# Convolution of the first two steps moved from VectorE and GpSimd to TensorE, with another order of all instructions

## The chip, the cores and the metric

The kernel runs on one core of one Trainium2 chip. The time is the device time of one execution in microseconds (us). Engines: PE is TensorE (PEld its weight loads), DVE is VectorE, ACT is ScalarE, POOL is GpSimd, SP is SyncE, whose queue issues nearly all transfers.

## The reference

Windowed attention with sinks, then a gated block with a causal convolution of five taps, all in float32. B = 4, H = 8, S = 768, head size 64, model size 512, 4 sinks, window 128.

```python
scores = where(is_sink | in_window, q @ k.T / 8, -1e9)
a = exp(scores - max(scores)); a = a / (sum(a) + 1e-9)
x = a @ v                                   # heads side by side: (B, S, 512)
gate_pre[s] = sum(conv_w[k] * x[s - 4 + k] for k in range(5))   # zeros ahead of s = 0
out = (sigmoid(gate_pre) * (x @ w_val)) @ w_out
```

w_val, w_out and conv_w arrive as float64 and are decoded on the chip into a high and a low float32 part.

## The kernel before

The work is cut into 24 steps s (batch, third of 256 positions, half of the heads) and 12 pairs m of two steps. A step's attention output is `xt`, 128 channels x 2 halves x 256 positions. What runs in which order on every engine is written out by hand: `ORDER` is a list of event names such as `s0.3` (name, then step, pair or weight chunk), and the program calls the function of each name in that order. Each engine runs its own instructions strictly in that order.

Events that matter here, with their lines in the kernel before: `kq`, `vv` load a step's k and q, and its v (L234 to L247); `wvl`, `wol` load a weight chunk, and `wva` to `wvf` decode it (ACT L135, L154, L149, L181, DVE, POOL L155, and three matmuls on PE, L176 to L178, the weight sum). `s0`, `s1` are the score groups of a step (PE L373, then DVE); `e0`, `e1` their exps on ACT (L397); `rec`, `norm` divide by the sums (POOL L412); `tx` transposes the probabilities (PE L434), `px`, `py` mask and copy them; `sk`, `ts` do the same for the sinks (PE L439); `vl`, `si` are the value products (PE L491, L500). `xc` copies the step's output from PSUM to `xt` (ACT L507), `xh`, `xl` make its high and low part. `c4` multiplies by the last tap (POOL L528), `hd` writes the four positions ahead of the tile into PSUM (ACT L519), `c0`, `c1` add two taps each (DVE L536, one instruction for each tap and half), `th` is the tanh (ACT L541). Per pair, `v0` to `v3` multiply with w_val (PE L555), `g`, `h`, `l` make the gated product and its parts, `o0` to `o3` multiply with w_out (PE L606), `t` stores. `fill` are dummy products of zeros on PE (L222), four in an event.

PSUM has two pairs of score banks, pr_86 and pr_87, used in turn by score groups and transposes (`pair`); two accumulators ac_92 and ac_93, used in turn by dummies, weight sums, sink transposes, `v` and `o` (`homes`); and one bank pair xv for the value products. A user waits until the last reader of its bank is done. For steps with p = 0 (the first two of a batch) the exps read a masked copy in SBUF (`sx`), for the others they read the score bank itself. `scalars` loads n_sink and window, `flag` tests them with eight small DVE operations; the result selects, after the main program, a general path that does not run here.

Of the kernel before, what the change touches and what calls it, by code (L numbers as in the profile page):

```python
# [41 lines left out]
sk.1 c1.0 wvf.2 wol.2 e1.3 ts.1 sk.2 px.2 vl.1 rec.3 th.0 woe.1 si.1 xc.1 xh.1 hd.1 wvd.3 s0.4 c4.1 wof.1 c0.1
fill.4g py.2 vv.10 wve.3 woa.2 ts.2 xl.1 woa.3 norm.3 e0.4 c1.1 s1.4 vv.2 wod.1 wvf.3 wob.2 v0.0 wob.3 v1.0 vv.5
tx.3 vl.2 vv.3 y0.0 th.1 v2.0 g0.0 hd.2 py.3 woe.3 h0.0 si.2 e1.4 l0.0 xc.2 v3.0 wod.3 o2.0 px.3 woe.2 y1.0 g1.0
c4.2 rec.4 kq.8 h1.0 wod.2 s0.6 xh.2 e0.6 wof.2 l1.0 s0.5 c0.2 o0.0 wof.3 c1.2 s1.6 o3.0 t1.0 e0.5 o1.0 xl.2 norm.4
sk.3 ts.3 vl.3 si.3 t0.0 kq.7 xc.3 xh.3 tx.4 hd.3 s1.5 sk.4 ts.4 px.4 e1.5 xl.3 v0.1 c4.3 v1.1 rec.5 py.4 v2.1 vv.4
c0.3 y0.1 th.2 c1.3 g0.1 e1.6 v3.1 y1.1 s1.7 s0.7 norm.5 th.3 vl.4 h0.1 l0.1 e1.7 si.4 tx.5 kq.9 rec.6 sk.5 xc.4
o0.1 kq.12 ts.5 g1.1 px.5 hd.4 s1.8 h1.1 o2.1 c4.4 l1.1 xh.4 c0.4 e0.7 o1.1 norm.6 xl.4 o3.1 t0.1 sk.6 vv.7 c1.4
rec.7 py.5 norm.7 tx.6 px.6 vl.5 e1.8 si.5 ts.6 t1.1 py.6 xh.5 xc.5 s0.9 s0.8 xl.5 vv.6 c4.5 sk.7 v0.2 hd.5 ts.7
th.4 e0.9 v1.2 sv.7 c0.5 v2.2 tx.7 c1.5 e0.8 rec.8 sv.6 g0.2 py.7 s1.9 px.7 v3.2 kq.10 th.5 vl.6 h0.2 s1.10 si.6  # L50
e1.9 norm.8 g1.2 xc.6 xh.6 hd.6 l0.2 rec.9 c4.6 tx.8 o0.2 vv.8 h1.2 l1.2 o2.2 xl.6 c0.6 py.8 c1.6 px.8 e1.10 o3.2
# [796 lines left out]
```

## Time and profile before

| | us |
|---|---|
| median of 3 runs (lowest, highest) | 268.03 (268.02, 268.99) |
| the profiled execution | 267.36 |
| its span in the profile | 265.6 |
| PE busy | 250.7 (94%) |
| DVE busy | 207.1 (78%) |
| ACT busy | 185.5 (70%) |
| POOL busy | 177.8 (67%) |

The span runs from the first to the last instruction that the profiler recorded; the execution's own time is 1.76 us longer. Matmuls are pipelined: a record's length includes the way through the array, so the time that one takes of PE is read from start to start of a long series, not from a record's length. A float32 matmul shows as two records.

### The profile page before, as it was taken

The numbers are of one execution on the slowest core, as the hardware profiler recorded it, in microseconds if no ns is written. First come the engines' busy times: TensorE is split into PE (matmuls) and PEld (weight loads), VectorE is DVE, ScalarE is ACT, GpSimd is POOL, SyncE is SP. The second block draws the span as 40 slices with busy tenths as digits, with TensorE's granted clock in tenths as the row PEclk, the third lists the DMA queues.
The fourth block names the chain that finished last, engine by engine and source line by source line (L and its number), as shares of the span: only waits on it lengthen the run. The fifth ranks groups of instructions, "written<-read, shape, count | busy, mean of one in ns | idle before, by whom it ended". The sixth has DMA issues, their size and how long they took to land. (4 is left out here: it accounts for less than half of the span.)

```text
span 265.6 us, 11978 instructions
## 1 busy us (share of the span) xinstructions
PE 250.7 (94%) x4978; PEld 207.6 (78%) x4978; DVE 207.1 (78%) x579; ACT 185.5 (70%) x686; POOL 177.8 (67%) x234
## 2 busy tenths in 40 slices
PE   7877999999999998999999999999999999999991
PEld 2345469769888877979888889999889889798991
DVE  6999999958979798888797878977689968953330
ACT  3899988868978767586657688587585566555131
POOL 3489987785696882885883786795692766676130
PEclk9999999999999999999999999999999999999999
DMA  6998771328335232763327636335055213020202
GB/s 203 329 364 236 246 264 39 127 86 265 107 118 168 63 122 84 251 228 116 89 79 232 211 99 207 94 107 165 9 160 174 63 42 102 2 81 2 81 3 88
DMA packets 27548, 36.57 MB, mean 138 GB/s; under 512 B 2272, under 2 KB 24032, under 8 KB 27488
## 3 DMA queue, kind: packets, MB, share of 16 engines
q1 hardware_dynamic: 27344, 35.62, 42.0%
q8 instruction: 41, 0.67, 1.1%
q14 instruction: 19, 0.16, 0.2%
q10 hardware_dynamic: 144, 0.13, 0.2%
HBM read 29.45 MB, written 6.29 MB: 135 GB/s over the span
## 5 line engine op out<-in xcount | busy, mean ns | idle before, releaser
L536 DVE SCALAR_TENSOR_TENSOR sg<-xv,cw,sg 128x256 f32<-128x256 f32 x192 | 77.7, 475 | 7.0 <-POOL sg L528 6.3
L412 POOL TENSOR_TENSOR wx<-w,sm 128x512 f32<-128x512 f32 x48 | 49.1, 1043 | 4.6 <-DVE sm L404 4.2
L555 PE MATMUL ac<-xh,wvh 128*128 128x256 f32 x192 | 49.5, 291 | 1.1 <-DVE pr L378 1.1
L584 POOL TENSOR_TENSOR gl<-sg,gh 128x512 fp32r<-128x512 f32 x24 | 30.9, 1291 | 29.1 <-ACT gh L580 29.0
L555 PE MATMUL ac<-xh,wvl 128*128 128x256 f32 x192 | 48.0, 283 | 0.0
L397 ACT ACTIVATE w<-pr,ngm 128x132 f32<-128x132 f32 x128 | 45.7, 369 | 1.7
L373 PE MATMUL pr<-k,q 64*32 64x168 f32 (+2 forms) x1536 | 36.7, 301 | 4.3 <-DMA q<-in_qt_dram 1.4
L528 POOL TENSOR_TENSOR sg<-xt,cw 128x512 f32<-128x512 f32 x24 | 25.5, 1063 | 20.8 <-ACT xt L507 20.7
L606 PE MATMUL ac<-woh,gh 128*128 128x512 f32 (+1 forms) x96 | 39.0, 406 | 0.0
L555 PEld LDWEIGHTS ac<-xh,wvh 128*128 128x128 f32 x192 | 36.9, 192 | 1.7 <-issue 0.5
L555 PEld LDWEIGHTS ac<-xh,wvl 128*128 128x128 f32 x192 | 36.7, 191 | 1.1 <-issue 1.0
L606 PE MATMUL ac<-wol,gh 128*128 128x512 f32 (+1 forms) x96 | 37.3, 388 | 0.0
L491 PE MATMUL xv<-wt,v 64*32 64x192 f32 (+2 forms) x2048 | 36.3, 275 | 1.0 <-PE ac L439 0.8
L606 PE MATMUL ac<-woh,gl 128*128 128x512 f32 (+1 forms) x96 | 37.2, 387 | 0.0
L491 PEld LDWEIGHTS xv<-wt,v 64*32 64x32 f32 x2048 | 33.7, 105 | 3.7 <-issue 1.5
L373 PEld LDWEIGHTS pr<-k,q 64*32 64x32 f32 x1536 | 23.9, 106 | 12.5 <-issue 3.2
L378 DVE COPY_PREDICATED pr<-low,pr 128x256 f32<-128x256 uint8 x48 | 20.3, 423 | 15.4 <-PE pr L373 14.5
L523 POOL TENSOR_TENSOR xl<-xt,xh 128x512 fp32r<-128x512 f32 x24 | 30.8, 1287 | 1.7 <-ACT xh L515 1.6
L555 PE MATMUL ac<-xl,wvh 128*128 128x256 f32 x192 | 30.9, 283 | 0.0
L555 PEld LDWEIGHTS ac<-xl,wvh 128*128 128x128 f32 x192 | 26.5, 192 | 0.0
L397 ACT ACTIVATE w<-sx,ngm 128x132 f32<-128x132 f32 x64 | 25.0, 400 | 1.9 <-DVE ngm L387 1.9
L397 ACT ACTIVATION_READ_ACCUMULATOR w<-pr,ngm 128x1 f32 x128 | 26.0, 203 | 0.0
(124 smaller groups left out, 460.6 us busy)
## 6 DMA issues: line engine op xcount, KB each, us to landing
k<-in_kt_dram SPq DMA_DIRECT2D x23, 408.0 KB, 5.3
v<-in_vt_dram SPq DMA_DIRECT2D x16, 384.0 KB, 4.5
q<-in_qt_dram SPq DMA_DIRECT2D x23, 256.0 KB, 5.3
out_dram<-osb SPq DMA_DIRECT2D x23, 256.0 KB, 2.6
raw<-in_w_val_dram SPq DMA_DIRECT2D x4, 512.0 KB, 5.8
v<-in_vt_dram SPq DMA_DIRECT2D x8, 256.0 KB, 3.9
raw<-in_w_out_dram SPq DMA_DIRECT2D x4, 512.0 KB, 5.9
vs<-in_vsk_dram SPq DMA_DIRECT2D x8, 64.0 KB, 3.5
```

The source lines that it names most:

```text
L373: nc.tensor.matmul(ss[e * QB:(e + 1) * QB, j, c * n + x0:c * n + x1], q[js, g, (4 * c + e) * QB:(4 * c + e + 1) * QB], k[js, g, (2 * c + e ...
L378: nc.vector.copy_predicated(sv[:, :, :, :D], low[:, None, None, :].to_broadcast([P, 2, 2, D]), sv[:, :, :, 2 * HB:])
L397: nc.scalar.activation(out=w[:, g, j, c], in_=sx[:, j, c, :PK], func=AF.Exp, scale=0.125 if steps[s][1] else -1.0, bias=ngm[:, g, j, c:c + ...
L412: nc.gpsimd.tensor_tensor(out=t[:, n].rearrange("p c h x -> p h c x"), in0=w[:, :, :, at], in1=sm.to_broadcast([P, 4, 2, D]), op=ALU.mult)
L491: nc.tensor.matmul(acc[r0:r0 + QB, g, x0 + h * D:x0 + (h + a1 - a0 + 1) * D], v[js, g, n, e * QB:(e + 1) * QB], t[js, n % 2, n // 2, g, a0 ...
L523: nc.gpsimd.tensor_tensor(out=half(xls, s, "xl", F32R), in0=xts[s], in1=half(xhs, s, "xh", F32R).bitcast(F32), op=ALU.subtract)
L528: nc.gpsimd.tensor_tensor(out=half(sg, s, "sg", F32), in0=xts[s], op=ALU.mult, in1=cw[:, g, KT - 1:].to_broadcast([P, 2, PQ]))
L536: nc.vector.scalar_tensor_tensor(out=g, in0=x, scalar=a, in1=g, op0=ALU.mult, op1=ALU.add)
L555: nc.tensor.matmul(acc[:, h], a[:, kc, cs], x[:, kc], start=(n == 0), stop=(n == 11))
L584: nc.gpsimd.tensor_tensor(out=gl, in0=g, in1=gh.bitcast(F32), op=ALU.subtract)
L606: nc.tensor.matmul(to, a[:, kc, ts], x[:, kc, cs], start=(kc + n == 0), stop=(kc + n == 5))
```

## The change

For steps 0 and 1 the convolution is done by PE: `dg` builds, on POOL, a diagonal 128x128 matrix for each tap and half (the identity times the tap's weights, all five taps of a half in one instruction of 640 columns, float32); `cf` and `cg` multiply xt of half 0 and 1 with the five diagonals, each product shifted by one position, and add them up in one accumulator; `th` reads its input there. The events c4, c0, c1 and hd of steps 0 and 1 are gone. The diagonals use the buffers of the gated products. The dummies come in twos, 20 events instead of 10, 40 products as before; and all 834 events stand in another order. `scalars` and `flag` stand later.

```diff
@@ ORDER (all its lines differ; one of each)
-load_conv masks signs fill.4a wvl.0 kq.0 wva.0 wvl.1 conv_weights wvb.0 s0.0 wvc.0 wvd.0 s1.0 wve.0 wvl.2 e0.0 wva.1
+load_conv masks fill.2g signs conv_weights kq.0 blanks fill.2i wvl.0 fill.2s fill.2e s1.0 fill.2b fill.2a wva.0
...
+    diag, cacc = {}, {}
+    def diagonals(qd):
+        diag[qd] = [p2.tile([P, KT, P], F32, name="diag", tag="gh" if h == 0 else "gl") for h in range(2)]
+        for h in range(2):
+            nc.gpsimd.tensor_tensor(out=diag[qd][h], in0=ident[:, None, :].to_broadcast([P, KT, P]), op=ALU.mult,
+                                    in1=cw[:, 2 * qd + h, :, None].to_broadcast([P, KT, P]))
+    def conv_first(s, h):
+        if h == 0:
+            cacc[s] = homes.pop(0).rearrange("p (h r) -> p h r", h=2)
+        acc, x = cacc[s][:, h], xts[s][:, h]
+        for kk in range(KT - 1, -1, -1):
+            w, n = diag[steps[s][2]][h][:, kk], KT - 1 - kk
+            nc.tensor.matmul(acc[:, n:], w, x[:, :PQ - n], start=(n == 0), stop=(kk == 0), skip_group_check=True)
+            if n and steps[s][1]:
+                nc.tensor.matmul(acc[:, :n], w, xts[s - 2][:, h, PQ - n:], start=False, stop=(kk == 0),
+                                 skip_group_check=True)
...
     def gate(s):
-        g = sg[s // 2][:, 2 * steps[s][2]:2 * steps[s][2] + 2]
-        nc.scalar.activation(out=g, in_=g, func=AF.Tanh, scale=0.5)
+        g = half(sg, s, "sg", F32)
+        nc.scalar.activation(out=g, in_=cacc.get(s, g), func=AF.Tanh, scale=0.5)
+        if s in cacc:
+            homes.append(cacc[s].rearrange("p h r -> p (h r)"))
...
+    acts |= {"dg": (diagonals, ()), "cf": (conv_first, (0,)), "cg": (conv_first, (1,))}
...
-    for n in "abcdefghijklmnop":
-        events["fill.4" + n] = busy, (4,)
+    for n in "abcdefghijklmnopqrstuvwx":
+        events["fill.2" + n] = busy, (2,)
```

The first place is PE around the first values of the program. Before, from step 2's transposes (L434) over the sink transposes of steps 1 and 2 (L439, with four dummies ahead that are left out here) to step 1's values (L491) and sinks (L500):

```order
L434 MATMUL pr_86<-ident,wx 128x64 x16
...
L439 MATMUL ac_92<-ident,skb_106 128x128
L439 MATMUL ac_93<-ident,skb_105 128x128
L491 MATMUL xv<-wt,v 32x192 x16
L491 MATMUL xv<-wt,v 32x128 x8
L491 MATMUL xv<-wt,v 32x64 x8
L500 MATMUL xv<-skt,vh 128x256 x2
```

In the new program, from step 3's second score group (L375) over step 0's values (L513) and sinks (L522), step 1's transposes (L436) and sink transpose (L441) to cf.0 (L493):

```order
L375 MATMUL pr_86<-k,q 32x168 x16
L513 MATMUL xv<-wt,v 32x192 x16
L513 MATMUL xv<-wt,v 32x128 x8
L513 MATMUL xv<-wt,v 32x64 x8
L522 MATMUL xv<-skt,vh 128x256 x2
L436 MATMUL pr_87<-ident,wx 128x64 x16
L441 MATMUL ac_93<-ident,skb_106 128x128
L493 MATMUL ac_92<-xt,diag 128x256
L493 MATMUL ac_92<-xt,diag 128x255
L493 MATMUL ac_92<-xt,diag 128x254
L493 MATMUL ac_92<-xt,diag 128x253
L493 MATMUL ac_92<-xt,diag 128x252
```

Step 0's values stood before step 1's transposes in both programs; what is new between those and step 1's values are the float32 products, and step 2's transposes come later. All 40 dummies stand ahead of cf.0; before, 36 stood ahead of step 1's values.

The second place is ACT ahead of the copy of step 0's output to xt. Before (L447 copies the sinks, L397 are step 2's exps, L507 is the copy, and step 3's exps follow):

```order
L403 ACTIVATE sm<-sm 128x8
L135 ACTIVATE wv_p<-raw 128x512
L149 ACTIVATE woh<-wo_t 128x512
L447 ACTIVATE skt<-ac_93,blk 128x128 x2
L394 ACTIVATE ngm<-ngm 128x4
L397 ACTIVATE w,sm<-pr_86,ngm 128x132 x4
L507 ACTIVATE xt<-xv 128x512
```

In the new program (L399 are the exps, of steps 2 and 3; L529 is the copy):

```order
L183 ACTIVATE wvl<-ac_93 128x4x128
L257 ACTIVATE vh<-vs 128x128
L396 ACTIVATE ngm<-ngm 128x4
L399 ACTIVATE w,sm<-pr_86,ngm 128x132 x4
L449 ACTIVATE skt<-ac_93,blk 128x128 x2
L405 ACTIVATE sm<-sm 128x8
L396 ACTIVATE ngm<-ngm 128x4
L399 ACTIVATE w,sm<-pr_87,ngm 128x132 x4
L183 ACTIVATE wvl<-ac_92 128x4x128
L529 ACTIVATE xt<-xv 128x512
```

The copy now stands behind one more exp group, step 3's first, and behind one more decode instruction in all. Ahead of it ACT has, in all, four exp groups that read sx, three that read a score bank, and thirteen decode instructions of 512 columns.

The third place is the end of DVE's work. Before (L449 is the last sink copy, L536 taps, L574 the gated products):

```order
L449 TENSOR_TENSOR skt<-ac_93,blk 128x256
L536 SCALAR_TENSOR_TENSOR sg<-xv,cw,sg 128x256 x4
L574 SCALAR_TENSOR_TENSOR sg<-sg,ac_92 128x512
L536 SCALAR_TENSOR_TENSOR sg<-xv,cw,sg 128x256 x4
L574 SCALAR_TENSOR_TENSOR sg<-sg,ac_93 128x512
```

In the new program (L558 taps, L106 to L117 the scalar test, L598 the gated products):

```order
L558 SCALAR_TENSOR_TENSOR sg<-xv,cw,sg 128x256 x4
L106 CAST nw_f<-nw_raw 128x4
L108 TENSOR_SCALAR nw<-nw_f 128x2
L109 TENSOR_TENSOR nw<-nw,nw_f 128x2
L110 TENSOR_SCALAR nw<-nw 128x2
L111 TENSOR_TENSOR nw<-nw,nw_f 128x2
L114 TENSOR_SCALAR flag<-nw 128x1 x2
L116 TENSOR_TENSOR flag<-flag 128x1
L117 CAST flag_i<-flag 128x1
L598 SCALAR_TENSOR_TENSOR sg<-sg,ac_93 128x512
L558 SCALAR_TENSOR_TENSOR sg<-xv,cw,sg 128x256 x4
L598 SCALAR_TENSOR_TENSOR sg<-sg,ac_92 128x512
```

Before, the test ran at 205.68 us; now it stands between step 23's first two taps and the last but one gated product.

## Rows read from the trace of the kernel before

**Rows 1.** The page: busy us, share of the span, instructions.

```profile
PE 250.7 (94%) x4978; PEld 207.6 (78%) x4978; DVE 207.1 (78%) x579; ACT 185.5 (70%) x686; POOL 177.8 (67%) x234
```

**Rows 2.** Stretches: length, busy PE, PEld, DVE, ACT, POOL (instructions), clock, DMA share, GB/s.

```profile
4.00:6.00 2.00, 1.61 (x4) 0.30 (x2) 0.63 (x4) 0.77 (x2) 0.00 (x0) 1.00 1.02 351
...
0.00:33.66 33.66, 26.63 (x428) 13.81 (x428) 29.64 (x103) 27.71 (x105) 23.88 (x44) 1.00 0.86 275
33.66:260.08 226.42, 224.08 (x4551) 193.77 (x4551) 177.47 (x477) 157.37 (x582) 153.94 (x192) 1.00 0.38 118
260.08:265.60 5.52, 0.00 (x0) 0.00 (x0) 0.00 (x0) 0.38 (x1) 0.00 (x0) 0.93 0.30 102
```

**Rows 3.** PE's waits from 39 to 260 us: total, times, longest.

```profile
PE ac L555 <- DVE pr L378: 1.1, 1, 1.1
...
PE pr L373 <- ACT w L397: 0.4, 1, 0.4
```

**Rows 4.** Timeline of PE: start us, us, line, shapes, count, idle before.

```profile
1.19 1.89 PE L207 MATMUL pr<-zero 128*128 128x512 bf16 x4 [1.19 <-DVE warm L759]
...
33.66 1.25 PE L491 MATMUL xv<-wt,v 64*32 64x192 f32 x64 [0.81 <-PE ac L439]
...
35.89 1.04 PE L222 MATMUL ac<-zero 128*128 128x512 bf16 x4
36.76 1.02 PE L176 MATMUL ac<-wv_t,ident 128*128 128x512 f32 x2
```

**Rows 5.** Timeline of PE, a weight sum and what follows it.

```profile
16.34 1.12 PE L176 MATMUL ac<-wv_t,ident 128*128 128x512 f32 x2
...
17.86 0.46 PE L434 MATMUL pr<-ident,wx 64*128 64x64 f32 x8
```

**Rows 6.** The chain that ended last: start us, us, what, records.

```profile
158.12 0.11 PE ac L439
158.23 0.64 PE pr L434 x16
...
162.38 5.74 PE ac L555 x48
```

**Rows 7.** Timeline of ACT in the start.

```profile
5.06 0.66 ACT L135 ACTIVATE wv_p<-raw 128x512 f32<-128x512 f32 x1 [3.05 <-DMA raw<-in_w_val_dram]
...
8.15 0.61 ACT L149 ACTIVATE wvh<-wv_t 128x512 fp32r<-128x512 f32 x1
8.70 0.41 ACT L397 ACTIVATE w<-sx,ngm 128x132 f32<-128x132 f32 x1
...
10.27 0.65 ACT L135 ACTIVATE wv_p<-raw 128x512 f32<-128x512 f32 x1
...
18.09 0.20 ACT L394 ACTIVATE ngm<-ngm 128x4 f32<-128x4 f32 x1
...
19.73 0.56 ACT L471 ACTIVATE wt<-pr 128x128 f32<-128x128 f32 x2
```

**Rows 8.** Lines 536 and 528: durations ns min/median/max, first and last start.

```profile
L536 DVE SCALAR_TENSOR_TENSOR sg<-xv,cw,sg x192: 431/474/485, 27.8 to 253.4; 128x256 f32<-128x256 f32 x192
L528 POOL TENSOR_TENSOR sg<-xt,cw x24: 1037/1044/1300, 26.8 to 245.4; 128x512 f32<-128x512 f32 x24
```

**Rows 9.** The page's transfers: count, KB each, median us from issue to landing.

```profile
k<-in_kt_dram SPq DMA_DIRECT2D x2, 204.0 KB, 3.7
q<-in_qt_dram SPq DMA_DIRECT2D x2, 128.0 KB, 3.7
```

**Rows 10.** Timeline of DVE: the first taps, the scalar test, the last gated products.

```profile
27.84 1.66 DVE L536 SCALAR_TENSOR_TENSOR sg<-xv,cw,sg 128x256 f32<-128x256 f32 x4
...
205.68 0.16 DVE L104 CAST nw_f<-nw_raw 128x4 f32<-128x4 int32 x1
...
207.97 0.42 DVE L449 TENSOR_TENSOR skt<-ac,blk 128x256 fp32r<-128x256 f32 x1
...
251.66 0.69 DVE L574 SCALAR_TENSOR_TENSOR sg<-sg,ac 128x512 f32<-128x512 f32 x1 [3.48 <-PE ac L555]
```

More of the change, by code (lines that the diff above doesn't have):

```diff
@@ L42 @@
[L42 to L51, printed above, removed]
@@ L77 @@
-v2.11 c0.23 g0.11 c1.23 h0.11 v3.11 l0.11 o0.11 th.23 g1.11 h1.11 l1.11 o2.11 o1.11 o3.11 t0.11 t1.11
+load_conv masks fill.2g signs conv_weights kq.0 blanks fill.2i wvl.0 fill.2s fill.2e s1.0 fill.2b fill.2a wva.0
+wvl.1 fill.2n wvb.0 dg.1 e1.0 s0.0 wvc.0 fill.2h kq.1 fill.2d kq.2 fill.2k wvd.0 wvl.2 vv.0 wva.1 fill.2p vv.1
+fill.2t e0.0 wve.0 wvb.1 wvc.1 s0.1 vv.2 rec.0 fill.2j wvf.0 e0.1 wvd.1 fill.2m s1.1 fill.2q wva.2 wol.0 s1.2 norm.0
+e1.1 e1.2 wvb.2 fill.2l tx.0 rec.1 dg.0 fill.2r wvc.2 woa.0 px.0 wvd.2 kq.3 wve.1 py.0 kq.6 fill.2o wol.1 fill.2c
@@ new lines @@
+s0.2 wvf.1 wvl.3 sv.0 e0.2 wve.2 wob.0 s0.3 norm.1 fill.2f sk.0 ts.0 rec.2 s1.3 norm.2 vl.0 e0.3 si.0 tx.1 wvf.2
+sk.1 px.1 xc.0 woe.0 e1.3 cf.0 kq.5 py.1 xh.0 sv.1 s1.6 ts.1 wva.3 rec.3 wof.0 vl.1 si.1 tx.2 kq.4 norm.3 vv.4 px.2
+wod.0 cg.0 wol.3 xh.1 sk.2 wvb.3 xc.1 py.2 vv.3 ts.2 woa.1 wvd.3 s0.4 xl.0 wvc.3 wob.1 s1.4 vl.2 cf.1 th.0 wve.3
+e0.4 woa.3 wvf.3 si.2 tx.3 wob.3 xl.1 v0.0 xc.2 hd.2 e1.4 kq.7 xh.2 v1.0 wod.3 woe.1 wol.2 y0.0 woe.3 cg.1 v2.0 px.3
+c4.2 e1.6 wod.1 g0.0 h0.0 c0.2 py.3 th.1 c1.2 v3.0 wof.3 woa.2 y1.0 wob.2 sk.3 ts.3 g1.0 woe.2 wod.2 wof.1 th.2 h1.0
@@ new lines @@
+g0.2 tx.7 e1.9 th.5 py.7 g1.2 h0.2 vl.6 px.7 rec.9 s1.10 hd.6 si.6 h1.2 l0.2 xc.6 tx.8 c4.6 kq.12 l1.2 sk.7 kq.11
+ts.7 o0.2 xh.6 o2.2 px.8 o3.2 c0.6 e1.10 py.8 c1.6 norm.9 t1.2 s0.12 s0.10 vl.7 si.7 tx.9 xl.6 th.6 xc.7 xh.7 c4.7
+kq.16 sk.8 ts.8 hd.7 px.9 c0.7 o1.2 c1.7 t0.2 xl.7 e0.10 v0.3 v1.3 sk.9 py.9 ts.9 s1.11 vl.8 si.8 g0.3 th.7 xc.8
+vv.9 s0.11 c4.8 hd.8 h0.3 l0.3 v2.3 xh.8 rec.10 c0.8 c1.8 v3.3 o2.3 g1.3 e1.11 s1.12 e0.11 h1.3 vl.9 rec.11 si.9
+norm.10 xc.9 tx.10 l1.3 o3.3 kq.13 px.10 o0.3 hd.9 vv.10 c4.9 xh.9 norm.11 c0.9 t1.3 sk.10 th.8 xl.8 ts.10 py.10
@@ new lines @@
+e0.12 vv.11 o1.3 sk.11 vv.12 c1.9 s0.13 vl.10 xl.9 ts.11 si.10 e1.12 t0.3 xc.10 tx.11 px.11 v0.4 rec.12 c4.10 v2.4
+hd.10 norm.12 th.9 xh.10 c0.10 c1.10 py.11 kq.14 v1.4 g0.4 e0.13 s1.13 h0.4 sv.12 vl.11 si.11 tx.12 e1.13 xh.11
+vv.19 px.12 l0.4 xl.10 xc.11 c4.11 sk.12 v3.4 ts.12 g1.4 kq.18 hd.11 py.12 s1.14 h1.4 rec.13 s0.14 e1.14 o2.4 c0.11
+e0.14 c1.11 l1.4 o0.4 kq.15 norm.13 o1.4 th.11 s0.18 s1.18 th.10 vl.12 tx.13 si.12 t0.4 py.13 xc.12 px.13 xl.11
+sk.13 xh.12 rec.14 o3.4 hd.12 t1.4 ts.13 s0.15 s1.15 v2.5 v0.5 e0.15 c4.12 e1.15 c0.12 v3.5 e0.18 norm.14 c1.12
@@ new lines @@
+xl.12 vv.13 v1.5 g1.5 sk.14 tx.14 kq.19 kq.17 sv.13 g0.5 vl.13 h0.5 vv.15 px.14 vv.14 ts.14 s0.16 rec.15 si.13
+scalars py.14 h1.5 l0.5 s1.16 xc.13 xh.13 c4.13 hd.13 c0.13 e0.16 e1.16 o2.5 l1.5 xl.13 c1.13 e1.18 o0.5 rec.16 o3.5
+th.12 norm.15 s0.17 sv.19 vl.14 si.14 t1.5 tx.15 xc.14 hd.14 sk.15 o1.5 vv.16 c4.14 py.15 ts.15 e0.17 norm.16 t0.5
+px.15 c0.14 v0.6 v1.6 g0.6 xh.14 kq.21 h0.6 l0.6 th.13 v2.6 c1.14 sk.16 s1.19 ts.16 s0.19 vl.15 xl.14 si.15 tx.16
+e1.19 v3.6 rec.18 kq.20 xc.15 g1.6 th.14 xh.15 o0.6 px.16 e0.19 py.16 warm_up c4.15 s1.17 h1.6 xl.15 v0.7 hd.15
@@ new lines @@
+e1.21 vv.21 sk.20 ts.20 h0.8 vl.19 s0.22 s1.22 l0.8 si.19 o2.8 xc.19 hd.19 c4.19 o3.8 xl.18 xh.19 xl.19 c0.19 o0.8
+th.18 c1.19 rec.21 e0.22 th.19 o1.8 e1.22 vl.20 s1.23 norm.21 t0.8 si.20 rec.22 tx.21 t1.8 v0.9 sk.21 px.21 xc.20
+ts.21 v1.9 hd.20 py.21 c4.20 c0.20 norm.22 v2.9 vv.23 g0.9 e1.23 v3.9 sk.22 c1.20 h0.9 g1.9 xh.20 s0.23 vl.21 ts.22
+si.21 h1.9 tx.22 xc.21 l0.9 hd.21 l1.9 c4.21 px.22 o0.9 xh.21 o2.9 vv.22 xl.20 c0.21 c1.21 o1.9 th.20 e0.23 o3.9
+xl.21 py.22 rec.23 norm.23 vl.22 th.21 tx.23 t0.9 si.22 hd.22 xc.22 v0.10 xh.22 t1.9 v1.10 v2.10 c4.22 px.23 c0.22
@@ L78 @@
+g0.10 xl.22 c1.22 py.23 v3.10 sk.23 g1.10 h0.10 vl.23 h1.10 l0.10 ts.23 si.23 xc.23 xh.23 o0.10 hd.23 l1.10 xl.23
+c4.23 c0.23 th.22 o1.10 v0.11 flag t0.10 v2.11 v1.11 v3.11 g0.11 h0.11 c1.23 th.23 l0.11 g1.11 h1.11 o2.10 o3.10
+o0.11 t1.10 l1.11 o1.11 o2.11 t0.11 o3.11 t1.11
 """
@@ L85 @@
 COPIES = 2
+PEC = (0, 1)
 def _iota_f32(nc, ti, tf, pattern, cm):
```

39 lines of the change are left out of this document (10 added, 29 removed).

## Prediction

> **What bounds the kernel now.** I read the page's table of engines first: PE is busy 250.7 us of 265.6 (94%) [rows 1]. An average can hide stages, so the second view is the table by stretches, cut where step 1's value products start (33.66 us) and where the last matmul ends (260.08) [rows 2]. The reader is to see three regimes. In the first stretch PE is idle 33.66 - 26.63 = 7.0 us, and 36 of the 40 dummy matmuls stand there too; four dummies take 36.76 - 35.89 = 0.87 us [rows 4], so 36 are 7.8 us or more. In the second, 226.42 us long, PE is idle only 2.3 us. In the last 5.52 us no matmul runs. The third view, PE's waits after 39 us, names 2.1 us of those 2.3: three waits [rows 3]. So PE's work is the bound from 33.66 us on; before that the bound is elsewhere, and PE has room.
>
> **The sum, from one point in both programs.** Take cf.0, the first convolution group. When PE reaches it in the new program (PE's fence in the section on the change), it has issued what the old one had issued at 33.66 us: eight score groups, three weight sums (L176 to L178), step 0's values and sinks, the transposes. The differences are small: all 40 dummies are done instead of 36, and step 2's transposes (0.64 us) and sink transpose (0.11 us) are not [rows 6]. So the PE time left after cf.0 starts is the old 226.4 us (waits included) - 0.87 + 0.75 + the four groups cf.0, cg.0, cf.1, cg.1. The new end of PE is the start of cf.0 plus that.
>
> Price of the groups: 4 x 5 = 20 products of 128x128 weights with 256 columns (a few with up to 4 fewer), both float32. Their nearest row is the float32 product of 512 columns in the weight sums, L176, which shows as two records. It and the two single-pass products after it last from 16.34 to 17.86 us, 1.52 us [rows 5]. A single pass of 256 columns takes 5.74 / 48 = 0.12 us [rows 6], so one of 512 about 0.24, and L176 is 1.52 - 0.48 = 1.04 us: four such passes and some 0.1 us of start. For 256 columns that is 4 x 0.12 = 0.48 us; I take 0.47, and 20 x 0.47 = 9.4 us. The bounds: half of 1.04, 0.52 us (10.4 in all), above; below, two records of one single pass each, 0.24 us (4.8 in all).
>
> PE time left is then 226.4 - 0.87 + 0.75 + 9.4 = 235.7 us. To end at the old 260.08, cf.0 would have to start at 24.4 us.
>
> **When cf.0 can start.** PE's own floor: the 26.63 us that it was busy before 33.66, + 0.87 - 0.75, after a first wait of 1.19 us for the zero tile [rows 4]: 27.9 us, without another wait. That is 3.5 us past the break-even, more than the 2.3 us of later idle could give back.
>
> ACT's floor: cf.0 reads xt of step 0, and ACT copies that (L507) behind a queue of its own (ACT's fence). Step 0's k and q, 2 x (204 + 128) = 664 KB, now stand ahead of the first w_val, at 351 GB/s [rows 2, 9]: 1.9 us, so ACT's first decode moves from 5.06 [rows 7] to 7.0 us. From there to xt ACT has four exp groups of masked scores at 10.27 - 8.70 = 1.57 us, three of plain scores at 19.73 - 18.09 = 1.64, thirteen 512-wide decode steps at 8.70 - 8.15 = 0.55, and some 2 us of small ones and the copy itself [rows 7]: 6.3 + 4.9 + 7.2 + 2 = 20.4, so 27.4 us if it never waits. It will: a score bank that step 1 or 2 needs is held until ACT's exps have read it (PE's score groups of steps 2 and 3 and tx.1 use the banks that e1.2, e0.2 and e0.3 hold). In the old start such waits show, 0.81 us at 33.66 [rows 4] being one. I take the later floor, 27.9, plus about one such wait, 0.9: 28.8 us.
>
> PE then ends at 28.8 + 235.7 = 264.5, 4.4 us later than 260.08; with the 5.52 us of the last stores [rows 2] the span is 270.0. The profiled execution took 267.36 us for a span of 265.6, 1.76 outside it: 271.8. The median of the runs shown, 268.03, is 0.67 above that execution: **272.5 us**, 4.4 us (1.7%) slower.
>
> **The parts that I cost at nothing.** DVE loses 16 tap instructions of 0.474 us, 7.6 us [rows 8]. The first of them started at 27.84 us [rows 10], so they held up nothing ahead of the point where cf.0 now stands; behind it PE is the bound. If PE were waiting for DVE later, up to 1.1 us would come back [rows 3]. POOL loses two products of 1.04 us and gains four diagonal builds of 640 columns, 1.04 x 640 / 512 = 1.3 us each by the nearest row [rows 8]; two stand ahead of the first wv_f, which waits for ACT anyway, two behind step 0's probabilities, ahead of the third wv_f. If that cover is gone, the third weight sum starts up to 2.6 us later, ahead of cf.0. ACT loses two head copies. The scalar test's eight small DVE operations take 207.97 - 205.68 = 2.3 us [rows 10]; they now stand ahead of the last-but-one gate product (DVE's fences). There DVE had idled 3.48 us, waiting for PE [rows 10], which hides them; uncovered they cost at most their 2.3 us. What is queued behind them on DVE are step 23's last two taps and the last gate product, and PE's last outputs wait for these. The order after cf.0 has no row that prices it: its waits lie between 0 and, say, twice the old 2.3 us; I keep 2.3.
>
> **A rule against the price.** The rows price a float32 product at four passes (1.04 us for 512 columns [rows 5]). The Trainium skill, Perfetto Trace Analysis, section Engine Utilization, puts the FP32_LOW_HIGH form at half of the array's output rate, two passes; its page FP8 and Floating Point Precision, TensorE Precision Notes, says four passes for true FP32. This trace agrees with the second. By the first the groups would cost half, which is the first rival.
>
> **Rivals.** (A) Float32 products at half price: each of the two records streams its 256 columns once, 0.24 us a product, 4.8 us in all. Place: the four groups. Then 272.5 - 4.6 = 267.9 us, not slower; it decides below about 0.31 us a product, where the time falls within 0.5% of before. For it: two records, not four. Against it: the 1.04 us. (B) The start gets worse: ACT's chain through the held banks, or the diagonals ahead of the third wv_f, put cf.0 at 31.8 us: 272.5 + 3.0 = 275.5. For it: ACT was busy 27.7 of the first 33.7 us [rows 2], and its queue now begins 1.9 us later. Against it: ahead of cf.0 DVE and ACT have nothing more to do than before, and PE has 40 dummies that fill small gaps. (C) The best the same price allows: cf.0 at PE's floor and no later wait: 272.5 - 0.9 - 2.3 = 269.3. For it: DVE has 7.6 us less to do, and the largest later wait is one for DVE [rows 3]. Against it: it needs every wait gone.
>
> **How the numbers follow.** Forecast 0.72, A 0.07, B 0.12, C 0.09. About 0.5% (1.3 us) is what a measurement can tell from no change, so 266.7 to 269.4 is "same". Faster: 0.03, from A with a good start. Same: the rest of A, half of C and a thin edge of the forecast, 0.12. Slower: 0.85. The range reaches down past C to 268.6 and up to B's 275.6.
>
> **What would show it.** In the new profile: 40 convolution records of about 0.22 us start to start, 9 to 10 us in all; the first of them at 28 to 30 us; no more than 3 us of PE idle behind it; the last matmul 3 to 6 us later than 260.08, and 5.5 us behind it as before. I am wrong if a product costs under 0.31 us, if cf.0 starts before 25 us, or if PE's work outside the four groups has shrunk.

## The result, and the profile of the changed kernel

The changed kernel takes 272.22 us (median of four executions, 271.03 to 273.5) against 268.27 of the kernel before: 1.0138 of its time, 95% interval 1.0097 to 1.018. The profiled execution took 272.1 us for a span of 270.0. A few executions of either kernel are over 1.5% longer than the fastest of the same kernel, and the ratios given here leave these out.

The page's table of engines, which answers to [rows 1] (busy us, share of the span, instructions):

```profile
PE 259.6 (96%) x5014; PEld 215.4 (80%) x5018; DVE 204.5 (76%) x563; ACT 185.7 (69%) x684; POOL 178.7 (66%) x236
```

PE is busy 8.9 us longer; some 1.7 us of that are the same work at half the clock (below). The table by stretches, cut at the first convolution product (28.52) and the end of the last matmul (265.40), answers to [rows 2]; columns are the window, its length, busy us and instructions of PE, PEld, DVE, ACT and POOL, the granted clock, and DMA:

```profile
0.00:28.52 28.52, 25.99 (x410) 12.85 (x414) 21.62 (x85) 22.01 (x86) 20.11 (x38) 1.00 0.91 303
28.52:265.40 236.88, 233.57 (x4605) 202.55 (x4604) 182.92 (x479) 163.28 (x598) 158.58 (x199) 0.99 0.37 117
265.40:270.00 4.60, 0.00 (x0) 0.00 (x0) 0.00 (x0) 0.38 (x1) 0.00 (x0) 0.72 0.21 66
```

Ahead of cf.0 PE idles 28.52 - 25.99 = 2.5 us, where the old start had 7.0. Four matmul records are missing from this stretch (410 beside 414 weight loads), so the 2.5 is somewhat too high: the profile of run 12 below has all 415 there, and 1.8 us. Behind it PE idles 3.3 us, and the wait list names nearly all of that (it answers to [rows 3]):

```profile
PE xv L513 <- issue: 2.1, 1, 2.1
PE pr L375 <- issue: 1.0, 1, 1.0
PE pr L436 <- DVE ngm L389: 0.2, 1, 0.2
```

No line names another engine for more than 0.2 us. "Issue" means that PE waited for nothing that the profile shows. PE's timeline of the groups (start, us, instruction), and of the long pause:

```profile
28.52 2.41 PE L493 MATMUL ac<-xt,diag 128*128 128x256 f32 x10
30.86 0.75 PE L375 MATMUL pr<-k,q 64*32 64x104 f32 x32
33.38 2.41 PE L493 MATMUL ac<-xt,diag 128*128 128x256 f32 x10
35.63 0.27 PE L441 MATMUL ac<-ident,skb 128*128 128x128 f32 x1
...
120.24 1.47 PE L513 MATMUL xv<-wt,v 64*32 64x64 f32 x80
123.85 0.35 PE L513 MATMUL xv<-wt,v 64*32 64x64 f32 x16 [2.15 <-issue]
```

cf.0 takes 30.86 - 28.52 = 2.34 us, cg.0 2.25; by the same view cf.1 takes 2.25 and cg.1 1.96: 8.8 us for 20 products, 0.44 each. The pause stands in the middle of step 10's values. What follows it shows in windows of 1 us:

```profile
122.00:123.00 1.00, 0.00 (x0) 0.00 (x0) 0.26 (x1) 0.00 (x0) 0.00 (x0) 1.00 0.20 76
...
124.00:125.00 1.00, 1.00 (x28) 0.91 (x20) 0.00 (x0) 0.24 (x1) 0.00 (x0) 0.54 0.75 220
125.00:126.00 1.00, 1.00 (x14) 0.88 (x11) 0.39 (x1) 1.00 (x4) 0.57 (x1) 0.50 1.02 374
126.00:127.00 1.00, 1.00 (x7) 1.00 (x6) 1.00 (x4) 0.60 (x3) 0.47 (x1) 0.50 1.04 278
127.00:128.00 1.00, 1.00 (x8) 1.00 (x8) 1.00 (x4) 1.00 (x5) 0.85 (x1) 0.76 0.38 112
```

From 122 to 123 us nothing runs but 0.26 us of DVE, and from 124 us on the granted clock is at half (the 1.2 GHz level) for 3.4 us, which loses about 1.7 us.

### The profile page after: what moved, and what is told of

Read it like the earlier page. It is cut to its first block, busy times and chain, and to the rows that moved or that the text cites. A ratio compares the mean times of both kernels' runs of the same rounds, so it can differ in the third digit from the quotient of the medians.

```text
span 270.0 us, 12052 instructions
## 1 busy us (share of the span) xinstructions
PE 259.6 (96%) x5014; PEld 215.4 (80%) x5018; DVE 204.5 (76%) x563; ACT 185.7 (69%) x684; POOL 178.7 (66%) x236
## 4 chain that ended last, share of the span: by engine, by line
PE 86%; ACT 5%; issue 3%; DMA 2%; POOL 1%; SPq 1%; DVE 0%; DVEq 0%
PE ac L579 27%; PE ac L630 25%; PE xv L513 11%; PE pr L375 10%; PE pr L436 5%; PE ac L493 3%; ACT w L399 3%; PE xv L522 3%; DMA raw<-in_w_val_dram 2%; PE ac L441 1%; POOL wx L414 1%; ACT wv_p L137 1%; ACT wv_p L156 1%; PE pr L630 1%; SPq L238 0%
## 5 line engine op out<-in xcount | busy, mean ns | idle before, releaser
L558 DVE SCALAR_TENSOR_TENSOR sg<-xv,cw,sg 128x256 f32<-128x256 f32 x176 | 71.4, 475 | 7.5 <-POOL sg L550 7.5
L579 PE MATMUL ac<-xh,wvh 128*128 128x256 f32 x192 | 50.5, 295 | 0.0
L608 POOL TENSOR_TENSOR gl<-sg,gh 128x512 fp32r<-128x512 f32 x24 | 31.0, 1290 | 27.4 <-ACT gh L604 26.8
L579 PE MATMUL ac<-xh,wvl 128*128 128x256 f32 x192 | 48.7, 285 | 0.0
L399 ACT ACTIVATE w<-pr,ngm 128x132 f32<-128x132 f32 x128 | 45.7, 369 | 1.6
L513 PE MATMUL xv<-wt,v 64*32 64x192 f32 (+2 forms) x2048 | 36.9, 275 | 2.1 <-issue 2.1
L550 POOL TENSOR_TENSOR sg<-xt,cw 128x512 f32<-128x512 f32 x22 | 23.1, 1049 | 23.1 <-ACT xt L529 22.8
L375 PE MATMUL pr<-k,q 64*32 64x168 f32 (+2 forms) x1536 | 36.7, 301 | 1.6 <-issue 1.0
L513 PEld LDWEIGHTS xv<-wt,v 64*32 64x32 f32 x2048 | 34.1, 105 | 4.8 <-issue 3.5
L579 PEld LDWEIGHTS ac<-xh,wvl 128*128 128x128 f32 x192 | 37.3, 194 | 0.1
L375 PEld LDWEIGHTS pr<-k,q 64*32 64x32 f32 x1536 | 23.2, 106 | 11.3 <-issue 5.1
L465 DVE TENSOR_TENSOR wt<-pr,cur 128x512 f32<-128x512 f32 x24 | 16.4, 685 | 15.6 <-PE pr L436 10.8
L399 ACT ACTIVATE w<-sx,ngm 128x132 f32<-128x132 f32 x64 | 25.0, 398 | 2.4 <-DVE ngm L389 2.4
```

Of the source, the lines that this page charges most:

```text
L375: nc.tensor.matmul(ss[e * QB:(e + 1) * QB, j, c * n + x0:c * n + x1], q[js, g, (4 * c + e) * QB:(4 * c + e + 1) * QB], k[js, g, (2 * c + e ...
L399: nc.scalar.activation(out=w[:, g, j, c], in_=sx[:, j, c, :PK], func=AF.Exp, scale=0.125 if steps[s][1] else -1.0, bias=ngm[:, g, j, c:c + ...
L465: nc.vector.tensor_tensor(out=t[:, :, :, a], in0=x[:, :, h0:], op=ALU.mult, in1=m[:, None, None, :].to_broadcast([P, 2, 4 - h0, D]))
L513: nc.tensor.matmul(acc[r0:r0 + QB, g, x0 + h * D:x0 + (h + a1 - a0 + 1) * D], v[js, g, n, e * QB:(e + 1) * QB], t[js, n % 2, n // 2, g, a0 ...
L550: nc.gpsimd.tensor_tensor(out=half(sg, s, "sg", F32), in0=xts[s], op=ALU.mult, in1=cw[:, g, KT - 1:].to_broadcast([P, 2, PQ]))
L558: nc.vector.scalar_tensor_tensor(out=g, in0=x, scalar=a, in1=g, op0=ALU.mult, op1=ALU.add)
```

## Experiments

In the diffs, names such as cf.0 are events of ORDER.

### 1. The changed kernel again

No edit.

> The changed kernel once more, to see what of its 4 us is always there. Theory (the time is matmul work added behind cf.0): cf.0 starts at 28.5 us again, the four groups take 8.8 us, the last matmul ends 4 to 5.5 us later than before, time 271 to 272.5 us. The first profile also showed a pause of PE of 2.15 us at 121.7 us with no wait behind it, next to a fetch of instructions, and 3.4 us at the lower clock after it (some 1.7 us lost). If that pause belongs to the new order (its place in the instruction stream), it stands within a few us of 121.7 again and the span is 270 again. Rival: it is a passing event; then it is gone or elsewhere, and the span is some 1 to 3 us below 270.0 where it is gone.

272.33 us, median of ten executions from 269.31 to 273.41, at 1.011 of before (1.0068 to 1.0152). cf.0 began at 28.70. The pause was there again, at 121.90 for 2.42 us, with three windows at half clock behind it, and the 0.9 us one at 221.3. So it belongs to the program, not to one execution; two executions have a profile, and both show it. The ten executions spread over 4 us; the profiled one is at 272.48.

### 2. Convolution back on DVE, in the new order

```diff
-... xc.0 woe.0 e1.3 cf.0 ... wod.0 cg.0 ... vl.2 cf.1 th.0 ... woe.3 cg.1
+... xc.0 hd.0 c4.0 c0.0 woe.0 e1.3 ... wof.0 c1.0 vl.1 ... xc.1 hd.1 c4.1 ... c0.1 c1.1 vl.2 th.0
```

> The new order, dummies by two and the late scalar test stay; the convolution of steps 0 and 1 goes back to DVE, ACT and POOL (no diagonals, no groups), right behind the copy of each step. Theory (groups cost PE 8.8 us): that much PE work goes; cf.0's place is then taken by step 1's values, which wait for ACT's copy and DVE's taps to free the bank, so 3 to 6 us of new PE idle stand between 28 and 45 us and the time is 266 to 269 us, at or below the kernel before. Rival (the new order of all is what costs the 4 us, the groups are hidden in PE's idle time): 271 to 273 us as in the changed kernel, with under 3 us of PE idle at the two places.

287.2 us, 1.0719 of before (1.0647 to 1.0791): neither theory. Waits of PE from 28 to 70 us:

```profile
PE xv L512 <- issue: 11.2, 2, 9.3
PE xv L512 <- DVE sg L557: 6.9, 1, 6.9
PE pr L374 <- ACT w L398: 1.8, 1, 1.8
```

The values of steps 1 to 3 wait 18 us for the bank that the taps of the step before still read. Two of these three waits carry the mark "issue", yet the longest of them ends at 54.53 us, just behind DVE's taps (54.44): the mark does not exclude a wait for another engine. Where the taps stand was my choice, so this is no clean undo. It shows that with the taps at these places the chain on DVE costs PE far more than 8.8 us; whether the new order has a better place for them was not tried.

### 3. Each product twice

```diff
+            nc.tensor.matmul(acc[:, n:], w, x[:, :PQ - n], start=False, stop=(kk == 0), skip_group_check=True)
```

> The changed kernel with each of the 20 float32 diagonal products issued twice into the same sum (the gate's input of steps 0 and 1 is doubled by it, so this output is not the reference's). Theory (0.44 us a product, nothing hides it): 20 x 0.44 = 8.8 us more, 280 to 281.5 us, and the groups take 17.6 us in the trace. Rival 1 (the products fill gaps of PE that would be idle in any case): less than 5 us more, 273 to 277 us. Rival 2 (products that repeat the same weights cost less, the weights being loaded): 4 to 7 us more.

280.86 us, 8.5 above the ten executions of run 1, and a span of 278.3. As the theory said: added products are paid in full, 8.5 / 20 = 0.43 us each. That the difference of the times fits so well is in part luck, since the pause at 121.7 and the half clock behind it are gone here, and pauses of 0.9, 1.3, 0.6 and 0.5 us stand at 43.2, 89.3, 165.1 and 182.7 instead. The price itself is seen in PE's timeline: the products of the first doubled group start 0.43 us apart.

### 4. The groups in a single pass

```diff
-        diag[qd] = [p2.tile([P, KT, P], F32, ...
+        diag[qd] = [p2.tile([P, KT, P], F32R, ...
-            nc.tensor.matmul(acc[:, n:], w, x[:, :PQ - n], ...
+            nc.tensor.matmul(acc, w, x, ...
```

> The four groups in one float32r pass instead of float32: the diagonals and the operand are rounded to float32r, and each of the five products covers all 256 columns without a shift (the low part of x and the shifts are left out, so this convolution is not the reference's). The rounded copy of step 0 stands ahead of cf.0. Theory: a product costs 0.12 us instead of 0.44, the groups 2.4 us instead of 8.8, so 6.4 us less: 265 to 266.5 us, faster than before by 1 to 3 us, with cf.0 0.3 to 0.6 us later because of the copy ahead of it. Rival (the order is the cost, or the products are hidden): 270 to 272.5 us.

The operand is the rounded copy of the step's output, which here stands ahead of cf.0, and all five products cover the same 256 columns. 272.06 us: the theory failed. The 20 products take 3.0 us start to start (0.15 each), so nearly 6 us of PE work went, and no time. Step 3's values start at 52.1 us, in the changed kernel at 51.8. Between cf.0 and that point PE now idles 22.91 - 18.73 = 4.2 us, where the changed kernel's PE was full:

```profile
29.19:52.10 22.91, 18.73 (x398) 15.55 (x399) 21.83 (x46) 20.34 (x69) 18.85 (x21) 1.00 0.43 141
```

```profile
28.52:51.80 23.28, 23.28 (x419) 20.36 (x419) 22.04 (x46) 20.27 (x69) 19.05 (x21) 1.00 0.45 144
```

The first row is of this run, the second of the changed kernel. DVE is busy 95% of it in both. PE's largest wait there is for ACT's tanh of the gate:

```profile
PE ac L440 <- ACT sg L562: 1.6, 1, 1.6
PE pr L374 <- ACT w L398: 0.8, 1, 0.8
PE ac L179 <- POOL wv_f L156: 0.6, 1, 0.6
```

cf.0 also starts 0.67 us later than in the changed kernel, behind the rounded copy (29.19). So PE and the others are bounds of nearly equal length from 28 to 52 us: in this order dearer groups cost in full, and cheaper ones give nothing.

### 5. Two loads earlier

```diff
-px.10 o0.3 hd.9 vv.10 c4.9 ... t1.3 ... e0.12 vv.11 o1.3 sk.11 vv.12 c1.9
+px.10 o0.3 hd.9 vv.10 vv.11 vv.12 c4.9 ... t1.3 ... e0.12 o1.3 sk.11 c1.9
```

> The changed kernel with two loads moved on SP alone: the v loads of steps 11 and 12, which were issued at 117.7 us behind a store that waits for ACT, stand ahead of that store and leave when their buffers come free (about 113 us). No engine's instructions change. It tests why PE paused 2.15 us at 121.7 us: in all three runs that have the pause, PE's instruction fetch began only when these loads had ended (121.57 in the first profile), and PE went on 2.3 to 2.5 us after it. Theory (the fetch waits behind the loads): the fetch starts 1 to 3 us earlier, the pause is gone or under 0.7 us, the clock does not fall behind it, and the time falls by 2 to 4 us, to 268 to 270 us. Rival (the fetch is late because of what PE itself issues, 150 products in 2 us, or belongs to its place in the stream): the pause stays at 2 us and the time at 271 to 273.

270.15 us (median of seven, 268.73 to 271.85), 1.0066 of before (1.0041 to 1.0091): 2.2 below run 1. In the profile, which is of the longest of the seven executions, the fetch (the arrival of PE's next instructions, last section) begins at 120.38, 1.2 us earlier, but the pause is still 1.60 us and half clock follows. So the loads are a part of it only. The time is where the theory had it, at its upper end, the pause is not.

### 6. The groups in the old order

```diff
-e0.2 norm.1 xc.0 ... c4.0 ... hd.0 ... wol.3 c0.0 ... c1.0 ... th.0
+e0.2 norm.1 xc.0 ... wol.3 cf.0 cg.0 th.0
```

Step 1 likewise; dg.1 stands behind conv_weights, dg.0 behind norm.0, each four dummies are two pairs.

> The order of the kernel before, with the float32 groups alone: cf, cg of steps 0 and 1 stand where the taps of the same steps stood, the diagonals behind conv_weights and norm.0, the dummies in the same places (as twos). Scalar test early, as before. Theory A (the groups are 8.8 us of PE work, of which only PE's idle time before 33 us can hide a part): 272 to 277 us. Theory B (the old start waits for ACT and DVE as much as the new one does in the run with short groups, where 6 us less of PE work gave nothing): most of the groups is hidden, 267 to 270 us, and then the new order of all, with the pause at 121.7 us, is what costs the 4 us.

289.6 us, 1.0809 of before (1.0774 to 1.0845), beyond both theories. The two groups of a step run as one block of 4.45 us, and DVE has nothing to do meanwhile:

```profile
33.00:36.00 3.00, 3.00 (x16) 2.66 (x15) 0.00 (x0) 0.37 (x2) 2.76 (x5) 1.00 0.01 3
```

PE also waits 2.5 us for POOL's wv_f, behind the diagonals. Pauses of 0.8 to 1.4 us with the mark "issue" stand at five later places, and the granted clock is 0.83 from 10 to 20 us. Up to its last matmul PE is busy 11.5 us longer than before (262.2 against 250.7) and idle 7.8 us longer. So in the old order, with the two groups of a step back to back, the groups are far from hidden; the new order puts scores and values between them.

### 7. Without dummies

All twenty fill events are taken out.

> The changed kernel without its 40 dummy matmuls (some 9 us of PE time ahead of cf.0). It tells what sets the start of cf.0. Theory of the prediction (PE's own floor, 27.9 us): cf.0 starts 4 to 8 us earlier unless the clock falls, and the time falls by as much, to 264 to 268 us. Rival (ACT's floor, 27.4 us, and the banks that ACT holds, lie just under it): cf.0 starts within 1 us of 28.5, PE is idle for 8 us instead, and the time stays at 270 to 273 us, or rises where PE's granted clock falls in the gaps.

270.54 us, 1.0086 of before (1.0059 to 1.0114): the time is within the rival's bounds, and cf.0's start is in neither's. It comes later, at 31.03, with 2 us of that in a pause at 27.7; without some 9 us of dummies PE is no earlier there. The clock falls in the gaps:

```profile
9.00:12.00 3.00, 1.68 (x3) 0.78 (x3) 2.86 (x14) 3.00 (x11) 0.83 (x1) 0.50 1.01 350
18.00:21.00 3.00, 2.74 (x13) 1.55 (x12) 2.86 (x4) 2.97 (x17) 2.83 (x6) 0.53 1.05 382
```

The time is made up later: at 121.7 us there is no pause in this run, and at the same number of PE instructions (below) one of 0.67.

### 8. Narrower dummies

```diff
-        for _ in range(n):
-            nc.tensor.matmul(t, zero[:, :P], zero, start=True, stop=True)
+        k = 6 if len(fills) % 5 < 3 else 7
+        c = n * 512 // k
+        for _ in range(k):
+            nc.tensor.matmul(t[:, :c], zero[:, :P], zero[:, :c], start=True, stop=True)
```

> The changed kernel with its 40 dummies of 512 columns cut into 128 of 146 to 170 columns: the same columns, so the same PE time, but 176 PE instructions more ahead of everything that follows. A fetch brings 16384 bytes, about 256 instructions by the records between two fetches, so the later program lies shifted in the fetched blocks by 176, which is the place it has in the run without dummies (80 fewer) that had no pause at 121.7 us. Theory (the pause is where a block of instructions ends in a dense stretch): cf.0 at 28.5 us as before, no pause over 0.8 us in 120 to 125 us, no stretch at half clock, PE end 262 to 263 us, time 268 to 270 us. Rival (the pause comes from the loads or from the step itself, wherever the blocks end): 1.5 to 2.4 us of pause in 120 to 125 us and 271.5 to 273 us.

272.22 us, the rival's time. Half right: no pause stands at 121.7, but one of 2.24 us now stands at 27.28, in step 0's values, and holds up cf.0 until 31.52; behind it three windows are at half clock. Cutting the dummies moved the pause.

### 9. Ten late dummies out

```diff
-fill.2l ... fill.2r ... fill.2o ... fill.2c ... fill.2f
```

> The changed kernel without the ten dummies behind 17 us (five of the twenty pairs), 2.2 us of PE time in the stretch in which ACT is busy without a break; the thirty before them stay, so the clock should stay at its upper level. Theory of the prediction's floor (PE's own work sets cf.0): cf.0 up to 2 us earlier, 270 to 271 us. Rival (ACT's queue sets it: the copy of step 0 ended at 28.47 us, cf.0 began at 28.52): cf.0 at 28.3 to 28.8 us with about 2 us more PE idle ahead of it, the same time as the changed kernel apart from the pause at 121.7 us, which may move with the 20 instructions fewer.

272.18 us (median of four): as the rival had it. cf.0 at 28.68, and PE idle ahead of it:

```profile
0.00:28.68 28.68, 23.71 (x402) 12.07 (x405) 21.86 (x85) 22.15 (x86) 20.19 (x38) 1.00 0.92 301
```

That is 28.68 - 23.71 = 5.0 us in place of 2.5, with cf.0 all but unmoved. What releases it is ACT's copy, first of the changed kernel, then of this run (ACT's timelines):

```profile
27.85 0.62 ACT L529 ACTIVATE xt<-xv 128x512 f32<-128x512 f32 x1
```

```profile
28.01 0.61 ACT L528 ACTIVATE xt<-xv 128x512 f32<-128x512 f32 x1
```

They end at 28.47 and 28.62, and cf.0 starts at 28.52 and 28.68. PE's largest waits ahead of it in this run are two for ACT's exps, 2.1 us together. ACT sets the start; the dummies lie in PE's spare time.

### 10. Narrower dummies and early loads

Edits 5 and 8 together.

> Both edits together: dummies cut into 128, and the two v loads ahead of the store. If the pause at 121.7 us has two causes that add (a fetch that waits behind loads, and the place of the block's end), this has the least of it: no pause over 0.5 us there, time 267.5 to 269.5 us, at the level of the kernel before. If the cut of the dummies alone removes it, this is equal to that run within 0.5 us.

271.52 us (270.28 to 272.9), equal to run 8 within 0.7: the theory's 267.5 to 269.5 failed. The profile has pauses of 0.7, 0.6 and 0.5 us at 32.7, 73.0 and 131.5. The one profile is among the shorter executions, so what the longer ones lose is not seen.

### 11. Two score groups moved away from the values

```diff
-e0.12 o1.3 sk.11 c1.9 s0.13 vl.10
+e0.12 s0.13 o1.3 sk.11 c1.9 vl.10
-vl.20 s1.23 norm.21 ... t1.8 v0.9 sk.21
+vl.20 norm.21 ... t1.8 v0.9 s1.23 sk.21
```

With the loads of run 5.

> The changed kernel with the two loads early, and two score groups moved on PE so that no score group stands next to a value group at the two places that paused in every run with this place in the stream: step 13's first scores ahead of four output rows (12 products of 512 columns) instead of right before step 10's values, and the last scores of step 23 behind the first value projection of step 9's pair instead of right behind step 20's values. Theory (PE consumes a fetched block of small products faster than the next can come, 2.3 to 2.9 us after the fetch begins): pauses at 121 and 220 us gone or under 0.5 us each, no half clock, some 3 to 4.5 us less than the profile with early loads alone: PE end 261 to 262 us, time 266.5 to 268.5 us, equal to the kernel before or faster by up to 0.6%. Rival (the pauses move on to the next dense place, as the one did that went from 121 to 27 us with narrower dummies): 1 to 2 us of pause elsewhere, time 269.5 to 271.5 us.

272.64 us. PE's waits from 110 to 232 us:

```profile
PE xv L513 <- issue: 2.0, 1, 2.0
PE ac L579 <- DVE skt L451: 1.2, 1, 1.2
PE ac L579 <- issue: 0.4, 1, 0.4
```

It looks like the rival, but the 2.0 us stand elsewhere: at the head of step 10's values, with DVE fully busy meanwhile. On DVE step 9's last taps (c1.9) now stood behind step 13's score reductions, and the values need the bank that these taps read; the taps end at 122.70 us, the values start at 122.79. A sink product on DVE came late in the same way. At the old two places 0 and 0.4 us were left.

### 12. The same, with DVE's order kept

```diff
-e0.12 o1.3 sk.11 c1.9 s0.13 vl.10
+e0.12 c1.9 s0.13 o1.3 sk.11 vl.10
-e0.22 th.19 o1.8 e1.22 vl.20 s1.23
+e0.22 th.19 s1.23 o1.8 e1.22 vl.20
```

With the loads of run 5. Against that run only PE's order differs.

> As the last run (two v loads early, two score groups away from the value groups beside them), but with the order of DVE, ACT, POOL and SP exactly that of the run with early loads alone: step 13's first scores ahead of one row of outputs (six products of 512 columns) behind step 9's last taps, and the last scores of step 23 ahead of the six output products that stood before step 20's values. In the last run the pauses at the two block boundaries (the 4745th and 8800th PE instruction) were gone or 0.4 us, but its other order on DVE made two real waits, 2.05 us for the taps of step 9 (the bank that step 10's values need) and 1.17 us for a sink transpose's product on DVE. Theory: with DVE's order kept both new waits stay away as well, pauses at the two places under 0.6 us, PE end 261 to 263 us, time 267 to 269.5 us. Rival (the block pauses stay when the scores are moved by a few us only): 1 us or more at one of the two places and 269.5 to 271 us.

267.82 us, median of twelve from 267.42 to 268.31: 0.9973 of before (0.9942 to 1.0004), no difference that can be told, and 4.5 us below run 1. The page's engines, and the stretches:

```profile
PE 258.7 (97%) x5018; PEld 213.9 (81%) x5018; DVE 204.4 (77%) x563; ACT 185.9 (70%) x684; POOL 178.8 (67%) x236
```

```profile
0.00:28.63 28.63, 26.83 (x415) 13.05 (x415) 21.44 (x85) 22.32 (x86) 20.16 (x38) 1.00 0.92 302
28.63:260.71 232.08, 231.91 (x4605) 200.86 (x4604) 182.97 (x479) 163.19 (x598) 158.66 (x199) 1.00 0.38 119
260.71:265.50 4.79, 0.00 (x0) 0.00 (x0) 0.00 (x0) 0.38 (x1) 0.00 (x0) 1.00 0.20 63
```

Behind cf.0 PE idles 0.2 us in 232. The clock never falls. The last matmul ends 4.45 us earlier than in run 5's profile (265.16), which is its two pauses, 1.60 + 1.27, and about 1.7 of half clock. (That profile is of run 5's longest execution; by the medians, 270.15 and 267.82, the gain is 2.3 us, and run 5's loads are the other 2.2 of the 4.5.)

## Why the prediction came out right, and which of its steps did not hold

The forecast was 272.5 us with a span of 270.0 and PE's end at 264.5; measured were 272.22, 270.0 and 265.4. Step by step:

- **cf.0's start**: 28.8 forecast, 28.52 found. PE's floor (27.9) and ACT's (27.4) stood close together in the sum; run 9 shows that ACT's queue decides. The forecast had built on PE's, so that it came near is owed to the two being close.
- **The price**: 0.47 us forecast, 0.44 found; 8.8 instead of 9.4. Doubling the products (run 3) confirms it. A single pass of 256 columns takes 0.12 us [rows 6], so these are nearly four, as the rows had it, and not two.
- **Later waits kept at 2.3 us**: this term failed in kind. Found were 3.3 us, with about 1.7 lost to half clock besides. The new order's own waits for other engines are 0.2. The rest is pauses at block ends of PE's instruction stream (last section), which no step of the sum had. Run 12 takes them away: against run 5 it changes PE's order alone, against the changed kernel also the two loads of run 5, and the slowdown is gone. It is the condition of rival C (no later wait), for which the forecast gave 269.3, and it took 267.82. The old trace had a sign of this. Of the three waits that the prediction counted as one sort, the one not printed in [rows 3] is no wait for another engine (the wait list, and the window up to it, whose second bracket counts the weight loads):

```profile
PE pr L373 <- issue: 0.6, 1, 0.6
```

```profile
0.00:58.92 58.92, 51.86 (x980) 33.42 (x980) 52.50 (x163) 48.40 (x174) 43.55 (x63) 1.00 0.64 211
```

  It stands in a score group, 980 weight loads in, and PE goes on at 59.52 us, 2.7 after an instruction packet starts (56.78): a pause of the same kind. The longest of the three, 1.1 us and put down to DVE's L378, may be one too: PE goes on at 106.50 us, 0.56 after that instruction had ended and 2.8 after a packet starts (103.74). ACT's last read of an accumulator ends at 106.28, so this is not settled; but rival C's reason, "the largest later wait is one for DVE", is weak.
- **The sum**: 235.7 us from cf.0 to PE's end forecast, 236.88 found: -0.6 for the price, +1.0 for the waits, +1.7 for the clock, and -0.9 that is spread over other groups and that I did not settle. The last stores took 4.60 us instead of 5.52, cause not looked for. That takes back PE's later end of 0.9 us, by luck: nothing in the forecast ties the two.
- **Rival A's price** (267.9 at half price, decided at 0.31 us a product) was wrong as a mechanism too: at 0.15 us (run 4) the time did not move, since from 28 to 52 us ACT and DVE bound as closely as PE does. "PE's remaining time" is a sum that could be added to here, but not subtracted from.
- **The parts costed at nothing** held. Of the scalar test, DVE's timeline near the end:

```profile
253.28 0.16 DVE L106 CAST nw_f<-nw_raw 128x4 f32<-128x4 int32 x1
...
254.72 0.15 DVE L117 CAST flag_i<-flag 128x1 int32<-128x1 f32 x1
255.55 0.69 DVE L598 SCALAR_TENSOR_TENSOR sg<-sg,ac 128x512 f32<-128x512 f32 x1 [0.68 <-PE ac L579]
```

  It is over 0.68 us before DVE has to wait for PE. POOL's diagonals made PE wait for no wv_f in the new order, but did in the old one (run 6).

So the balance of the change itself, from before to run 12: PE has 8.0 us more to do (250.7 [rows 1] to 258.7), and 7.4 us less idle time up to its last matmul (260.1 - 250.7 = 9.4 before, 260.7 - 258.7 = 2.0 there). The added work fills time in which PE had waited: neutral. Run 12 has the new order of all events and the two loads in it as well, so this is the balance of the whole change; no run separates the groups from the order, since the groups in the old order (run 6) and the taps in the new one (run 2) both make waits of their own. The 4 us of the changed kernel are the pauses and the clock. The number was right for a reason that was half wrong: that PE's work bounds the time behind cf.0 held, and what made this program slower than before was a term that the sum did not have.

## What to carry to other kernels

Work added to the busiest engine is not simply added: look whether it fills that engine's waits (halve it as well as double it), and put it where other engines have work meanwhile. When an order is changed, look in the profile for waits marked "issue" on an engine with thousands of small instructions, and count its instructions up to each: if the count is the same in different orders, suspect the instruction stream rather than a late producer, and try another order of that engine around the place. The mark alone is not enough: in runs 2 and 11 it stood on waits for a bank that DVE still read. And move an instruction group on one engine at a time: the same idea cost 2.5 us (run 11 against 5) or gained 2.3 (run 12), by what stood behind it on DVE.
